# Quads of heads: K and Q loaded in rows of 1,024 and 1,536 bytes, token order restored on chip, bounds in three column groups, and a new order of the work

## The chip, the cores and the metric

The kernel runs on one core of one Trainium2 chip. The metric is device time in microseconds (us). The core has five engines with instruction queues of their own: TensorE (PE in the profile; PEld is its weight load), VectorE (DVE), ScalarE (ACT), GpSimd (POOL) and SyncE (SP). Data comes from device memory (HBM) into the on-chip memory (SBUF, 128 partitions) through 16 DMA engines that are started by DMA instructions in a queue, nearly all of them in SP's. TensorE writes its results to PSUM.

## The reference, cut to what matters

Four batches, eight heads, 768 tokens, head size 64. Keys are grouped in 24 chunks of 32 tokens. For each query and each chunk an upper bound of the score is formed from the chunk's smallest and largest key; the six chunks with the highest bounds (among those that do not lie in the future) are kept, and ordinary causal softmax attention runs over the kept chunks. The result goes through a two-layer block with a hard-swish between the layers.

```python
k_min, k_max = np.min(k_chunks, axis=3), np.max(k_chunks, axis=3)          # chunks of 32 tokens
ub = np.sum(np.maximum(q[:, :, :, None, :] * k_min[:, :, None, :, :], q[:, :, :, None, :] * k_max[:, :, None, :, :]), axis=-1)
top_chunks = np.argsort(np.where(causal, ub, -1e9), axis=-1)[..., -6:]
scores = np.where(sel & (pos[:, None] >= pos[None, :]), scale * np.matmul(q, k.transpose(0, 1, 3, 2)), -1e9)
attn_out = softmax(scores) @ v                                             # (4, 8, 768, 64)
h = x @ w_in                                                               # x: (3072, 512), w_in: (512, 2048)
out = (h * np.clip(h + 3, 0, 6) / 6) @ w_out                               # (3072, 512) float32
```

A query's first six chunks need no choice, so for the first 192 tokens of a head no bounds are computed.

## The kernel before

Everything is written into one list of tokens, `ORDER`, a hand-over from a planner: each token names an operation and its arguments, and the program issues them from left to right. Each engine works off its own tokens strictly in this order; a token that has to wait holds up all later tokens of the same engine. The list is thus five queues in one.

**Pairs and quads.** Heads are processed in pairs i = 0 to 15 (two heads, four pairs per batch). Pairs 0 to 3 (the first batch) take one path, written with capital letters: K and Q arrive in halves (`LK`, `LQ` on SP, `AQ` on ACT's queue, 96 KB each), are turned by TensorE against an identity matrix (`KT`, `QT`), cast (`KB`, `QB`) and reduced to chunk bounds (`MX`, `MN`); `UH`, `UB`, `TH`, `T8`, `SE`, `LH`, `MT` give the selection. Pairs 4 to 15 are taken as quads n = 2 to 7 (four heads, two pairs each), written with small letters, and these are what the change is about:

- `lk.n`, `lq.n` (line 222, SP): load K or Q of four heads into a third of `STAGE`, 768 KB. Head g of the quad goes to partitions 32g to 32g+31; a row of one token (64 floats, 256 bytes) is one piece. Four DMA instructions, one for each head.
- `kd`, `qd` (line 228, DVE): transpose 32x32 blocks in place, in two halves of 128x768. Afterwards a partition holds one of 32 dimensions and the free axis runs over chunk n, half x of the head size and token t.
- `kb`, `qb` (line 303, ACT): cast to bfloat16 into `KBA`, `QBA`, two instructions of 128x768 each. `mx`, `mn` (line 311, DVE): the largest and smallest key of each chunk, two instructions each. `kx` (line 316, DVE): largest minus smallest. `rp` (line 322, ACT): the positive part of Q.
- `ud` (line 333, PE): the bounds, as 64 float32 matmuls on 32x32 tiles: two operands w (positive part, raw Q), two halves x, four column groups `part` of 144 queries, four heads g. The results stand in 128 partitions (4 groups of 32 chunks) by 144 queries. Each matmul shows as two records.
- `us` (339), `tr` (343), `tm` (350, nine instructions per half quad), `se` (353), `tb` (357), all DVE: add the causal bias, transpose, find the eight largest of each list, compare with the sixth, transpose back. `mv` (line 363, POOL): 16 copies per quad gather the mask of each head into one row block `MQ`.
- `SQ` (lines 510 and 514, PE): scores of a quad; line 510 multiplies K by Q, line 514 adds the mask with a matmul whose moving operand is read from `MQ` in runs of eight.
- `ex` (520, ACT) and `af` (527, POOL): exponent and causal cut; `A`, `B` (543, PE) multiply by V, loaded by `LV` or `lv` (SP) and cast by `VC` or `vc` (POOL); `na`, `nb` (560, 563, DVE) normalise into `XB`.

**The block behind it.** A group of 384 tokens is transposed either by TensorE (`X`, line 576) and copied by DVE (`xe`, 580), or by DMA (`xt`, 569); groups 0 to 2 take the first way, groups 3 to 7 the second. `H` (587, PE) is a piece of the first layer, eight matmuls of 384 columns; `hu` (595, ACT) and `gt` (598, DVE) form the hard-swish; `O` (625, PE) is a quarter of a tile of the second layer, four matmuls of 512 columns; `ot` (632, ACT) and `st` (636, SP) bring it out. The weights come in eight loads of 1 MB (`wl`, line 238, SP) into two buffers `WS` in turn and are cast by POOL (`wc`, 242), so `wl.2` waits for `wc.0` and so on.

**Queues around the change.** On SP the tokens from the first quad load on are, before:

```
lk.2 LV.3.0.0 LK.3.1.1 LV.0.0.1 LV.1.0.1 LQ.3.1.0 LV.1.0.0 LQ.3.1.1 LV.2.0.0 LV.2.0.1 LV.0.1.1 wl.0 wl.1 LV.0.1.0 LV.1.1.1 LV.1.1.0 wl.2 lk.3 wl.3 lq.2 LV.3.1.0 LV.3.1.1 LV.2.1.1 LV.2.1.0 wl.4 lq.3 wl.5 wl.6 lv.5 wl.7 lk.4 lq.4 lv.4 st.0.0 lv.7 st.0.1 st.0.2 lv.6 lk.5 lv.8 st.1.0 lq.5
```

On PE the first quad's bounds `ud.2` stand behind all scores and value products of pairs 0 to 3 and all of `H.0`; `ud.3` behind `H.1` but two pieces; `ud.4` behind `A.4`.

Of the kernel before, what the change touches and what calls it, by code (L numbers as in the profile page):

```python
# [15 lines left out]
P = 128  # L16
CH = 32
# [17 lines left out]
PW AQ.2.0.1 LK.0.0.0 PT PI PO LK.0.1.1 AQ.0.0.1 PR Z.y.6 PZ PF PB LK.0.0.1 KT.0.0.b PC AQ.0.0.0 MX.0.0 EG.2 LK.1.0.1  # L35
MN.0.0 EG.0 LK.1.0.0 PA EG.1 QT.0.0.y AQ.1.0.1 EG.3 AQ.1.0.0 LK.0.1.0 AQ.2.0.0 RP.0.0 RN.0.0 KT.1.0.a MN.1.0 MX.1.0
KB.0.0 QB.0.0 QT.1.0.x KT.0.1.y RP.1.0 KB.1.0 RN.1.0 UH.0.0.c UH.1.0.b QB.1.0 MN.0.1 KB.0.1 LQ.0.1.1 UB.1.0 UB.0.0
MX.0.1 LQ.0.1.0 QT.0.1.a RA.0.1 QB.0.1 RP.0.1 TH.1.0.b T8.1.0 TH.0.0.c LQ.3.0.1 T8.0.0 QT.2.0.x RP.2.0 SE.1.0
LQ.3.0.0 QT.3.0.y RP.3.0 LK.3.0.0 RN.2.0 SE.0.0 LK.2.0.1 UH.0.1.a LK.2.0.0 KT.2.0.b RN.3.0 LK.3.0.1 UB.0.1 QB.2.0
MN.2.0 QB.3.0 KT.3.0.c LQ.2.1.0 KB.3.0 LH.1.0.a MX.2.0 MT.1.0 KB.2.0 LQ.2.1.1 QT.2.1.y UH.2.0.a RP.2.1 RA.2.1 QB.2.1  # L40
MX.3.0 LK.3.1.0 LH.0.0.b MN.3.0 TH.0.1.x LQ.1.1.1 MT.0.0 S.0.1.b ex.0.1 UB.2.0 T8.0.1 SE.0.1 S.0.0.a ex.0.0 LK.1.1.0
af.0.0 LQ.1.1.0 QT.1.1.c RN.1.1 QB.1.1 TH.2.0.y RP.1.1 LH.0.1.b LK.1.1.1 KT.1.1.x T8.2.0 SE.2.0 UH.3.0.a LH.2.0.y
MT.0.1 LV.3.0.1 KB.1.1 LV.0.0.0 LK.2.1.1 S.1.1.b UB.3.0 ex.1.1 af.1.1 MT.2.0 MN.1.1 S.0.5.c LK.2.1.0 MX.1.1 KT.2.1.y
MN.2.1 MX.2.1 S.1.0.a TH.3.0.x ex.0.5 ex.1.0 UH.1.1.b T8.3.0 S.2.1.c SE.3.0 UB.1.1 UH.2.1.a UB.2.1 af.0.5 LH.3.0.b
MT.3.0 TH.1.1.x af.0.1 ex.2.1 KB.2.1 af.2.1 T8.1.1 S.2.0.c TH.2.1.y af.1.0 ex.2.0 lk.2 LV.3.0.0 S.0.3.b ex.0.3
S.0.4.c SE.1.1 T8.2.1 SE.2.1 LH.1.1.x MT.1.1 LK.3.1.1 ex.0.4 LV.0.0.1 VC.0.0 KT.3.1.a MN.3.1 A.0.y LV.1.0.1 na.0
# [646 lines left out]
```

## Time and profile before

| what | us |
|---|---|
| time, median of 2 runs (276.49 to 276.76) | 276.62 |
| the profiled execution, its own time | 275.69 |
| its span, first to last instruction | 274.0 |
| PE busy | 261.3 (95%) |
| DVE busy | 184.0 (67%) |
| ACT busy | 181.0 (66%) |
| POOL busy | 102.6 (37%) |
| SP's DMA queue, share of 16 engines | 56.6% |

Busy time is the time that an engine's records cover. The profile's groups give line, engine, operation, tile, shape and count, then busy time, mean nanoseconds of one, and the idle time before the group with what ended it. The chain is followed back from the last instruction to what released it. A stretch (window) gives each engine's busy time in it, the granted clock, the mean busy share of the 16 DMA engines and the GB/s that they moved. The granted TensorE clock is 1.000 all through.

### The profile page before, as it was taken

To read this page: it belongs to the slowest core of one execution; us is meant where nothing else is said; L and a number is where in the kernel's file an instruction comes from. 1 tells how busy PE (TensorE), PEld (TensorE's weight loads), DVE (VectorE), ACT (ScalarE), POOL (GpSimd) and SP (SyncE) were. 2 spreads that over 40 slices of the span, in tenths; PEclk is the share of its full clock that TensorE was granted. 3 is DMA by queue.
4 is the path that set the end of the run, shared out by engine and by line. 5 is a ranking of instruction groups with operands and counts; after the bars stand their busy time and mean duration, and the time that the engine had idled before them with its cause. 6 is when DMAs were issued, how large, how long until landed. Compare 5 with 4: busy or idle time off the path is not lost.

```text
span 274.0 us, 8574 instructions
## 1 busy us (share of the span) xinstructions
PE 261.3 (95%) x3550; PEld 153.7 (56%) x3550; DVE 184.0 (67%) x452; ACT 181.0 (66%) x249; POOL 102.6 (37%) x241
## 2 busy tenths in 40 slices
PE   6998997899999999999999999998999999999994
PEld 3666765565545565664545655464655565555561
DVE  4898998999899779867874788575662423342620
ACT  2798978647499894878578746992887634325610
POOL 7215686325777552532825232421544310000000
PEclk9999999999999999999999999999999999999999
DMA  8999999998996999139900449114212044003002
GB/s 164 205 180 163 335 250 252 219 286 246 261 184 190 160 212 186 36 76 171 231 4 28 107 103 173 40 21 99 79 52 47 2 133 100 0 2 115 38 22 97
DMA packets 91479, 36.08 MB, mean 132 GB/s; under 512 B 84144, under 2 KB 84400, under 8 KB 91440
## 3 DMA queue, kind: packets, MB, share of 16 engines
q1 hardware_dynamic: 89040, 34.94, 56.6%
q10 hardware_dynamic: 2400, 0.59, 1.2%
q8 instruction: 28, 0.46, 0.8%
q14 instruction: 11, 0.09, 0.1%
HBM read 27.26 MB, written 6.29 MB: 122 GB/s over the span
## 4 chain that ended last, share of the span: by engine, by line
PE 76%; DMA 13%; SPq 3%; DVE 3%; POOL 1%; ACT 1%; issue 1%; DVEq 0%
PE PSy L625 15%; PE PSx L625 10%; PE PBa L587 10%; PE PBc L587 9%; PE PBb L587 8%; DMA WS<-in_moe_w_in_dram 4%; DMA STAGE<-in_q_dram 4%; DMA STAGE<-in_k_dram 3%; PE PBa L510 3%; PE PSx L543 2%; PE PSy L543 2%; PE PBc L625 2%; PE PBc L510 2%; PE PBb L510 2%; PE PBb L333 2%; DMA XT<-XB 1%
## 5 line engine op out<-in xcount | busy, mean ns | idle before, releaser
L587 PEld LDWEIGHTS <-WIN 128*128 128x128 bf16 x512 | 48.9, 98 | 37.7 <-issue 4.2
L527 POOL TENSOR_SCALAR_AFFINE_SELECT PT<-PT 128x256 bf16<-128x256 bf16 x78 | 30.2, 409 | 70.2 <-ACT PT L520 69.9
L625 PEld LDWEIGHTS <-GT 128*128 128x128 bf16 x368 | 33.1, 98 | 37.8 <-issue 2.4
L625 PE MATMUL PSy<-WOUT,GT 128*128 128x512 bf16 x192 | 46.8, 380 | 0.0
L363 POOL COPY MQ<-MTM 32x144 bf16<-32x144 bf16 x96 | 29.1, 304 | 31.3 <-DVE MTM L357 27.5
L587 PE MATMUL PBc<-XT,WIN 128*128 128x384 bf16 x184 | 33.7, 326 | 1.4 <-DVE GT L598 1.4
L598 DVE SCALAR_TENSOR_TENSOR GT<-U,PBa 128x768 bf16<-128x768 bf16 x22 | 20.9, 948 | 19.8 <-ACT U L595 19.8
L587 PE MATMUL PBa<-XT,WIN 128*128 128x384 bf16 x176 | 32.4, 326 | 1.3 <-DMA XT<-XB 0.7
L625 PE MATMUL PSx<-WOUT,GT 128*128 128x512 bf16 x128 | 31.8, 380 | 0.0
L598 DVE SCALAR_TENSOR_TENSOR GT<-U,PBc 128x768 bf16<-128x768 bf16 x23 | 21.8, 947 | 10.4 <-ACT U L595 10.3
L520 ACT ACTIVATE PT<-PBb 128x1024 bf16<-128x1024 f32 (+2 forms) x26 | 23.6, 908 | 7.6 <-PE PBb L514 5.3
L587 PE MATMUL PBb<-XT,WIN 128*128 128x384 bf16 x152 | 27.8, 326 | 0.2 <-POOL WIN L242 0.2
L595 ACT ACTIVATE U<-PBc 128x768 bf16<-128x768 f32 x23 | 18.7, 812 | 13.9 <-PE PBc L587 10.2
L598 DVE SCALAR_TENSOR_TENSOR GT<-U,PBb 128x768 bf16<-128x768 bf16 x19 | 18.1, 951 | 13.6 <-ACT U L595 13.6
L595 ACT ACTIVATE U<-PBa 128x768 bf16<-128x768 f32 x22 | 17.9, 812 | 13.5 <-PE PBa L587 13.5
L520 ACT ACTIVATE PT<-PBc 128x1024 bf16<-128x1024 f32 (+2 forms) x26 | 24.2, 930 | 3.5 <-PE PBc L497 1.3
L520 ACT ACTIVATE PT<-PBa 128x1024 bf16<-128x1024 f32 (+2 forms) x26 | 23.9, 921 | 3.8 <-PE PBc L514 2.0
L228 DVE STREAM_TRANSPOSE STAGE<-STAGE 128x768 f32<-128x768 f32 x24 | 22.7, 960 | 1.7 <-DMA STAGE<-in_k_dram 1.3
L595 ACT ACTIVATE U<-PBb 128x768 bf16<-128x768 f32 x19 | 15.4, 812 | 12.1 <-PE PBb L587 12.1
L311 DVE TENSOR_REDUCE KMA<-STAGE 128x24 f32<-128x768 f32 x24 | 22.3, 941 | 0.1
L543 PEld LDWEIGHTS <-PT 128*128 128x128 bf16 x546 | 19.0, 97 | 3.6 <-issue 0.7
L510 PEld LDWEIGHTS <-KBA 32*128 32x128 bf16 x480 | 9.4, 92 | 14.7 <-issue 11.7
(192 smaller groups left out, 460.3 us busy)
## 6 DMA issues: line engine op xcount, KB each, us to landing
out_dram<-OT SPq DMA_DIRECT2D x23, 256.0 KB, 2.5
STAGE<-in_k_dram SPq DMA_DIRECT2D x24, 192.0 KB, 5.0
STAGE<-in_q_dram SPq DMA_DIRECT2D x24, 192.0 KB, 5.5
VS<-in_v_dram SPq DMA_DIRECT2D x12, 384.0 KB, 4.2
WS<-in_moe_w_in_dram SPq DMA_DIRECT2D x4, 1024.0 KB, 7.0
WS<-in_moe_w_out_dram SPq DMA_DIRECT2D x4, 1024.0 KB, 6.7
STAGE<-in_k_dram SPq DMA_DIRECT2D x16, 96.0 KB, 3.2
VS<-in_v_dram SPq DMA_DIRECT2D x16, 96.0 KB, 4.2
```

The lines of the kernel that those rows point to most:

```text
L228: nc.vector.transpose(out=T, in_=T)
L311: nc.vector.tensor_reduce(out=dst, in_=staged("k", n)[:, h], axis=AX.X, op=(A.max, A.min)[w])
L333: nc.tensor.matmul(PSB[(c, cc)[g // 2]][CH * part:CH * (part + 1), g % 2, 0:NQ // 4], lhsT=KM4[n % 2][rows, w, x, :], rhs=R[rows, :, x, 8 ...
L363: nc.gpsimd.tensor_copy(MQ[n % 2][CH * g:CH * (g + 1), w * part:w * (part + 1)], MT4[n % 2][CH * part:CH * (part + 1), w * g:w * (g + 1)])
L510: nc.tensor.matmul(PSB[both[g // 2]][:, g % 2, at:at + w], lhsT=K[rows, x, j * P:(j + 1) * P], rhs=Q[rows, x, q0:q0 + w], start=(x == 0), ...
L520: nc.scalar.activation(pt(i, u)[:, :, 0:n], PSB[slot["S", i, u]][:, :, 0:n], ACT.Exp, scale=float(scale))
L527: nc.gpsimd.affine_select(out=T[:, :, lo:lo + P], in_=T[:, :, lo:lo + P], pattern=[[0, 2], [1, P]], compare_op=A.is_ge, fill=0.0, base=0, ...
L543: nc.tensor.matmul(O[:, e, t, :], lhsT=pt(i, u)[:, e, lo:lo + P], rhs=VB[i % 4][:, j, e, :], start=(j == 0), stop=(j == qb))
L587: nc.tensor.matmul(PSB[c][:, ff, 0:GRP], lhsT=WIN[:, kt, (2 * f + ff) * P:(2 * f + ff + 1) * P], rhs=XT[g % 3][:, kt, :], start=(kt == 0), ...
L595: nc.scalar.activation(slot["R", g, f][:], PSB[slot["H", g, f]][:, :, 0:GRP], ACT.Relu, bias=3.0)
L598: nc.vector.scalar_tensor_tensor(out=GT[g % 2][:, 2 * f:2 * f + 2, :], in0=slot["R", g, f][:], scalar=6.0, in1=PSB[slot["H", g, f]][:, :, ...
L625: nc.tensor.matmul(PSS[c], lhsT=GT[g % 2][:, f, t * P:(t + 1) * P], rhs=WOUT[:, f, :], start=(f == 0), stop=(f == FT - 1))
```

## The change

It is made for quads only, but for three things that touch the pairs of the first batch or the end: the late half of the pairs' bounds is laid out anew, group 2 is transposed by DMA (`xt.2` in place of `X.2.0`, `X.2.1`, `xe.2.0`, `xe.2.1`), and the list `ORDER` is another permutation of the same tokens.

- **Loads.** `RUN` says how many consecutive tokens form one piece: 4 for K (1,024 bytes), 6 for Q (1,536 bytes). A DMA instruction takes, for one u, 32 pieces of each of four heads, and writes all 128 partitions: 6 instructions for K and 4 for Q in place of 4 and 4, with 128 pieces each. Its source runs over heads (4), then pieces (32), then the row; its destination over 128 partitions, then the row.
- **Token order.** After the transposes the free axis runs over u, r (which token of the piece), x and t. `kb`, `qb` read it with r innermost, at a step of 64 floats, and become four instructions of 128x384 each; `mx`, `mn` read runs of eight tokens for each r and become four instructions each.
- **Bounds.** `ud` has three column groups of 192 queries, 48 matmuls; `us`, `tr`, `se`, `tb` run on 96 partitions by 384 in place of 128 by 288; `tm` has twelve instructions per half quad; `mv` is 12 copies of 32x192 per quad and restores token order for Q (reads at a step of 32); line 514's counterpart reads `MQ` in one run.
- **Pairs, late half.** `UH.i.1` is 16 matmuls of 96 columns in four groups in place of 8 of 192, `UB` one add of 128x192 in place of 64x384, `TH` two transposes in place of four.
- **Order.** On SP, from the first quad load on, after:

```
lk.2 LQ.3.1.0 LQ.3.1.1 wl.0 LV.0.0.0 LV.0.0.1 LV.2.0.0 LV.1.0.1 LV.1.0.0 LV.3.0.1 LV.2.0.1 LV.3.0.0 lk.3 LV.0.1.1 LV.1.1.1 LV.0.1.0 wl.1 LV.1.1.0 wl.2 wl.3 LV.3.1.1 LV.2.1.1 LV.2.1.0 lq.2 LV.3.1.0 wl.4 lq.3 wl.5 wl.6 lv.5 wl.7 lq.4 lk.4 lv.4 lk.5 lv.7 st.0.0 st.0.2 lv.6 lq.5
```

On PE, `ud.2`, `ud.3` and `ud.4` stand behind the same work as before, in another sequence.

```diff
+    RUN = {"k": 4, "q": 6}
+    NP3 = NQ // 3
...
+    def slab(m, n):
+        at = (1 + 2 * (n - FIRST_QUAD) + "kq".index(m)) % 3
+        return FLAT[:, 2 * S * at:2 * S * (at + 1)]
+
     def staged(m, n):
-        at = (1 + 2 * (n - FIRST_QUAD) + "kq".index(m)) % 3
-        return STAGE[:, 2 * at:2 * at + 2].rearrange("p h (n x t) -> p h n x t", x=2, t=CH)
+        return slab(m, n).rearrange("p (u r x t) -> p x u r t", r=RUN[m], x=2, t=CH)
...
     def load_rows(m, x):
-        def issue(n, *only):
+        def issue(n):
             b, first = divmod(4 * n, H)
-            dst = staged(m, n).rearrange("p h n x t -> p (h n) (x t)")
-            for g in only or range(4):
-                nc.sync.dma_start(dst[CH * g:CH * (g + 1)], x[b, first + g].rearrange("(n t) d -> t n d", t=CH))
+            r = RUN[m]
+            dst = slab(m, n).rearrange("p (u y) -> p u y", y=r * D)
...
+                src = x[b, first:first + 4].rearrange("g (u t r) d -> u g t (r d)", t=CH, r=r)
+                for u in range(S // (CH * r)):
+                    nc.sync.dma_start(dst[:, u], src[u])
...
     def to_bf16(m, engine):
         def issue(n, h):
...
+                for x in range(2):
+                    copy(dst[:, x, us], staged(m, n)[:, x, us].rearrange("p u r t -> p u t r"))
...
     def chunk_bounds(w):
         def issue(n, h):
-            dst = KM4[n % 2][:, w, :, NCH // 2 * h:NCH // 2 * (h + 1)].rearrange("p x n -> p n x")
-            nc.vector.tensor_reduce(out=dst, in_=staged("k", n)[:, h], axis=AX.X, op=(A.max, A.min)[w])
...
+            for x in range(2):
+                nc.vector.tensor_reduce(out=dst[:, x].rearrange("p (u c) -> p u c", c=c),
+                                        in_=src[:, x, us * h:us * (h + 1)].rearrange("p u r (c t) -> p u c r t", c=c),
+                                        axis=AX.XY, op=op)
...
     def bounds(n, c, cc):
...
-                for part in range(4):
+                for part in range(3):
                     for g in range(4):
                         rows = slice(CH * g, CH * (g + 1))
-                        nc.tensor.matmul(PSB[(c, cc)[g // 2]][CH * part:CH * (part + 1), g % 2, 0:NQ // 4],
-                                         lhsT=KM4[n % 2][rows, w, x, :], rhs=R[rows, :, x, 8 * part:8 * part + 8],
+                        R = raw[rows, x, 6 * part + 6:6 * part + 12] if w else RPA[rows, x, NP3 * part:NP3 * (part + 1)]
+                        nc.tensor.matmul(PSB[(c, cc)[g // 2]][CH * part:CH * (part + 1), g % 2, 0:NP3],
+                                         lhsT=KM4[n % 2][rows, w, x, :], rhs=R,
...
     def top8(n, p):
-        for s in range(9):
-            nc.vector.max(out=T8D[:, 9 * p + s, :], in_=bounds_rows(p)[:, s, :])
+        for s in range(12):
+            nc.vector.max(out=T8D[0:96, 12 * p + s, :], in_=bounds_rows(p)[:, s, :])
...
     def gather_rows(n, g):
-        for part in range(4):
-            w = NQ // 4
-            nc.gpsimd.tensor_copy(MQ[n % 2][CH * g:CH * (g + 1), w * part:w * (part + 1)],
-                                  MT4[n % 2][CH * part:CH * (part + 1), w * g:w * (g + 1)])
+        for part in range(3):
+            lo = NP3 * part
+            src = MT3[(2 * n + g // 2) % 3][CH * part:CH * (part + 1), NP3 * (g % 2):NP3 * (g % 2 + 1)]
+            dst = MQ[n % 2][CH * g:CH * (g + 1), lo:lo + NP3]
+            if RUN["q"] > 1:
+                src, dst = src.rearrange("p (r t) -> p t r", t=CH), dst.rearrange("p (t r) -> p t r", t=CH)
+            nc.gpsimd.tensor_copy(dst, src)
...
     def bounds_half(i, h, c):
-        n = 96 * (h + 1)
         for m, R in enumerate((RP, RN)):
-            for g in range(2):
-                lo = Q0 * h + n * g
+            for g in range(2 * (h + 1)):
+                lo = first_query(h, g) - Q0
...
     def scores_quad(n, u, *both):
-        chosen = MQ[n % 2][:].rearrange("p (r n t) -> p n r t", r=4, t=8)
...
-                                 rhs=chosen[rows, (lo - Q0) // CH:(q0 + w - Q0) // CH], start=False, stop=True,
+                                 rhs=MQ[n % 2][rows, lo - Q0:q0 + w - Q0], start=False, stop=True,
```

More of the change, by code (lines that the diff above doesn't have):

```diff
@@ L108 @@
+O.7.2.2.y O.7.2.3.y ot.7.2 st.7.2 st.7.1 st.7.0
 """.split()
@@ L284, in zero_masks @@
         nc.vector.memset(EM[:], 0.0)
[L285 removed]
+        nc.vector.memset(BIAS3[:], 0.0)
     def spread(g):
@@ L366, in bias_quad @@
     def bias_quad():
-        for g in range(4):
-            T = BIAS4[CH * g:CH * (g + 1)]
-            nc.gpsimd.affine_select(out=T, in_=T, pattern=[[1, NQ // CH], [0, 8]], compare_op=A.is_ge, fill=-1e9,
-                                    base=TOPK, channel_multiplier=-1)
+        for g in range(3):
+            T = BIAS3[CH * g:CH * (g + 1)]
+            nc.gpsimd.affine_select(out=T, in_=T, pattern=[[1, 6], [6, CH]] if RUN["q"] == 6 else [[CH, 6], [1, CH]], compare_op=A.is_ge, fill=-1e9,
+                                    base=Q0 * (g + 1), channel_multiplier=-CH)
```

253 lines of the change are left out of this document (132 added, 121 removed).

## The prediction

> **What bounds the kernel now.** I read the page first (busy time, DMA queues), then stretches of the span, then the chain of waits in the stretch that the change touches.
>
> ```profile
> PE 261.3 (95%) x3550; PEld 153.7 (56%) x3550; DVE 184.0 (67%) x452; ACT 181.0 (66%) x249; POOL 102.6 (37%) x241
> ...
> q1 hardware_dynamic: 89040, 34.94, 56.6%
> q10 hardware_dynamic: 2400, 0.59, 1.2%
> ```
>
> PE is covered for 261.3 of 274.0 us: only 12.7 us can be won by filling it. The stretches show where those are (columns: busy time of PE, PEld, DVE, ACT, POOL with counts, granted clock, DMA share, GB/s):
>
> ```profile
> 0.00:16.80 16.80, 13.17 (x133) 8.57 (x134) 12.03 (x52) 9.54 (x23) 7.14 (x17) 1.00 0.96 182
> 16.80:52.30 35.50, 31.83 (x489) 21.84 (x488) 32.70 (x89) 29.22 (x40) 21.05 (x38) 1.00 1.01 235
> 52.30:69.90 17.60, 17.17 (x272) 10.84 (x269) 16.98 (x40) 11.35 (x17) 8.03 (x13) 1.00 0.96 259
> 69.90:89.20 19.30, 19.30 (x328) 9.99 (x330) 17.32 (x44) 14.84 (x21) 14.53 (x36) 1.00 0.94 217
> 89.20:113.20 24.00, 24.00 (x444) 14.55 (x444) 20.50 (x53) 18.97 (x26) 9.08 (x23) 1.00 0.88 165
> 113.20:274.00 160.80, 155.83 (x1898) 87.86 (x1896) 84.43 (x177) 97.07 (x128) 42.77 (x117) 1.00 0.33 74
> 250.00:260.00 10.00, 10.00 (x62) 5.87 (x60) 5.88 (x7) 6.83 (x9) 0.00 (x0) 1.00 0.28 105
> ```
>
> Up to 52.3 us the DMA engines are taken all the time (0.96, 1.01) and PE is not; from there to 89.2 both are full; after 113 the DMA share is 0.33. So **the first 52 us belong to the DMA queue**, and from then on PE sets the pace. The chain of waits has the hand-over:
>
> ```profile
> 42.00 0.59 SPq L222
> ...
> 44.62 7.67 DMA STAGE<-in_q_dram
> ...
> 52.42 0.98 DVE STAGE L228
> ...
> 54.16 0.97 DVE STAGE L228
> 55.13 0.02 issue
> 55.15 0.53 ACT RPA L322
> 55.68 0.04 issue
> 55.73 0.31 PE PBc L333 x2
> ...
> 57.74 0.46 PE PSx L576 x6
> ```
>
> `lq.2`, the first Q quad, lands at 52.29; two transposes and the positive part later, `ud.2` starts at 55.73. From landing to start: 3.44 us. The other two marks that I need are the starts of `ud.3`, `ud.4` and `ud.5` on PE, and the DVE work from the first transpose of K's third quad to its span (`kd.4.1` to `kx.4`):
>
> ```profile
> 69.92 0.31 PE L333 MATMUL PBb<-RPA,KMA 32*32 32x144 f32 x2
> ...
> 89.16 0.31 PE L333 MATMUL PBb<-RPA,KMA 32*32 32x144 f32 x2
> ```
>
> ```profile
> 114.17 0.31 PE L333 MATMUL PBb<-RPA,KMA 32*32 32x144 f32 x2
> ```
>
> ```profile
> 80.71 0.93 DVE L228 STREAM_TRANSPOSE STAGE<-STAGE 128x768 f32<-128x768 f32 x1
> ...
> 87.98 0.46 DVE L316 TENSOR_TENSOR KMA<-KMA 128x48 f32<-128x48 f32 x1
> ```
>
> **The change part by part. Loads.** A quad load is 786,432 bytes. Up to 16.8 us only 256-byte rows are moved: 182 / 0.96 = 190 GB/s, 11.9 for each of 16 engines. From 250 to 260 us only stores, in 2,048-byte rows: 105 / 0.28 = 375 GB/s, 23.4 for each. So a quad load costs 4.1 us of all engines now, and longer rows on 16 engines would cost 2.1 to 4.1.
>
> But on how many engines does it run? ACT's queue q10 answers that for the transfers of before: it carries six half loads of 384 rows, 2,304 packets, and shows 2,400. The 96 left are 16 for each load, one closing packet per engine; the outermost size of those loads is 128 on both sides. The quad loads of before have 32 outermost on both sides. The new ones have **four heads outermost in the source** and 128 partitions in the destination. If shares are cut along the outermost size, four shares can be made, and a load lies on four engines while twelve stand by. No row shows a load with so small an outermost size, so both ends stay: 16 engines (2.1 to 4.1 us) or four, 196,608 bytes each, 8.4 us at the 23.4 GB/s of 2,048-byte rows, 16.6 at the 11.9 of the short ones. I take four engines and 9.0 us, near the long rows.
>
> The Trainium skill ("DMA: Bandwidth & Descriptors", section "Why a DMA increments its semaphore by 16 and not by 1") says that a DMA is spread over the largest count up to 16 that divides the slowest dimension of both sides, on the lowest-numbered engines. By that rule it is four engines, the same four each time; the 16 closing packets above agree with it for 128, and no run here shows it for four.
>
> *Step A, `ud.2`.* Three quad loads (`lk.2`, `lk.3`, `lq.2`) lie before 52.3 in a queue that is never empty: 3 x (9.0 - 4.1) = 14.7 us on the engines that end last. `LV.3.1.1`, `LV.2.1.1`, `LV.2.1.0` now stand ahead of `lq.2`: 98,304 bytes at 190 GB/s, 0.5 each, 1.6. `lq.2` lands at 52.3 + 16.3 = 68.6, `ud.2` starts at 72.0. The work ahead of `ud.2` on PE is the same set of operations as before and was done at 55.7, so nothing covers the wait: **+16.3**. Weights and V are spread over all engines, so their shares on the four end behind the quad loads too; `H.0` gets its weights later by as much, and no work is left over to fill in.
>
> *Step B, `ud.4`.* After `lq.2` come one V half (0.5), four weight loads (2.8 each at 375 GB/s, 11.2), `lv.5` (2.1) and three quad loads (27.0): `lk.4` lands at 109.4. From 80.71 to 88.44 DVE needed 7.7 us for transposes, reductions and span; with eight half-size reductions some 8.3. `ud.4` can start at 117.7. Pushed by step A alone it would stand at 89.16 + 16.3 = 105.5: **+12.2** more. `ud.3` between them isn't late: `lq.3` lands at 68.6 + 0.5 + 2.8 + 9.0 = 80.9, `ud.3` starts at 69.92 + 16.3 = 86.2. Nor is `ud.5`: `lk.5` and `lq.5` (18.0), three `lv` (6.3) and two stores (1.4) end at 135.1, plus 3.4, against 114.17 + 28.5 = 142.7. Behind it a quad takes over 30 us of PE and 18 of the four engines, and the share was 0.33: hidden.
>
> *What is queued behind the loads.* On SP:
>
> ```profile
> L222 SPq DMA_DIRECT2D STAGE<-in_k_dram x24: 311/520/2432, 15.3 to 126.6; - x24
> ```
>
> ```profile
> 81.27 0.37 SPq L636 DMA_DIRECT2D out_dram<-OT  x1
> ```
>
> Twelve more DMA instructions at 0.31 to 0.52 are 4 to 6 us of SP in the whole run, four of them before `lq.2`: 2.1, behind a queue that isn't empty, so nothing. At the end `st.7.1` now follows `st.7.2`: one issue more behind the last tile, +0.4. On DVE `kd.2.0` now stands ahead of the selection of pairs 1 to 3 and waits for `lk.2` (issued near 17, landed near 27); up to 3 us of DVE and then PE, covered by the wait for `lq.2`, which ends at 72. `kd.5.1` stands ahead of `us.4` and waits for `lk.5` (120.5): 1 to 2 us, covered by pieces of `O`. Without these covers both would add their time.
>
> **The engines' own work.**
>
> ```profile
> L363 POOL COPY MQ<-MTM 32x144 bf16<-32x144 bf16 x96 | 29.1, 304 | 31.3 <-DVE MTM L357 27.5
> ...
> L311 DVE TENSOR_REDUCE KMA<-STAGE 128x24 f32<-128x768 f32 x24 | 22.3, 941 | 0.1
> ...
> L350 DVE MAX8 T8D<-UBT 128x8 f32<-128x32 f32 x108 | 11.0, 176 | 0.3
> ...
> L303 ACT CAST KBA<-STAGE 128x768 bf16<-128x768 f32 x12 | 9.9, 832 | 0.0
> ...
> L343 DVE STREAM_TRANSPOSE UBT<-UBM 128x288 f32<-128x288 f32 x12 | 5.6, 466 | 0.1
> ...
> L288 POOL COPY EM<-XT 32x768 bf16<-32x768 bf16 x4 | 3.3, 818 | 0.2
> ...
> L412 DVE TENSOR_REDUCE KMA<-PSy 128x12 f32<-128x384 f32 x4 | 2.1, 553 | 0.3 <-PE PBc L440 0.3
> ...
> L576 PE MATMUL PSx<-IDENTB,XB 128*128 128x128 bf16 x12 | 1.0, 221 | 0.0
> ...
> L405 ACT CAST KBA<-PSy 128x384 bf16<-128x384 f32 x2 | 1.0, 476 | 0.3 <-DVE KMA L412 0.3
> ```
>
> ```profile
> L510 PE MATMUL PBb<-QBA,KBA 32*128 32x384 bf16 x88 | 10.9, 326 | 0.0
> ...
> L514 PE MATMUL PBb<-MQ,EM 32*128 32x384 bf16 x36 | 5.9, 321 | 0.0
> ```
>
> - DVE: 24 reductions of 941 ns become 48 of about 553: +3.9 us. Four kinds of 12 instructions go from 288 to 384 columns; by the transpose (466 ns at 288, 0.93 us at 768 in the rows above) that is 0.1 each, +4.8. `tm` 108 to 144 at 11.0 / 108: +3.7. About +12 of 184, spread over 200 us, beside matmuls. Of it 1.2 lies before 57 us, under the DMA.
> - ACT: 24 casts of 832 become 48 of 476 to 832 (a step of 64 floats isn't in the trace; contiguous, or twice the price per element): +2.9 to +20 of 181. I take the lower; a cast is not on the way to `ud`.
> - POOL: 72 copies for 96 of 304 ns (29.1 us in all); by the 818 for 768 columns, 343 each, 24.7; at twice that, 49: still half of POOL idle, and 16 us of PE work stand between bounds and mask.
> - PE: the mask reads in one run, but reading runs of eight was no dearer (321 beside 326): 0. The bounds have the same column count, 64 x 144 = 48 x 192, and took 57.7 - 55.7 = 2.0 us: from 3/4 (priced by instruction) to 4/3 (12 tiles in flight in place of 16), -3 to +4 in six quads; I take 0. `X.2` goes: two times six transposes of 0.5, -1.0.
> - The late quads let `gt` and `ot` catch up where DVE was 90% busy: -1.0, an estimate.
>
> **Sum.** 275.69 + 16.3 + 12.2 + 0.4 - 1.0 - 1.0 = 302.6 for the profiled execution; the median stood 0.9 above it: 303.5, **303** as a round number. At 8.4 us a load both steps give 24.9, 300; with step B hidden 289; at 11 us 40.5, 316. Its own range is 289 to 316.
>
> **Rivals.** *All 16 engines, DVE takes over (within 2%).* Three loads of about 2.5 save 4.8 before `lq.2`, V takes 1.6 back; but DVE is busy for 32.70 of 35.5 us there and gets 1.2 more, so 1.6 to 3.2 remain, and 1.0 of `X.2`: about 273. For it: the queue's share of 1.01. Against it: the four heads outermost.
> *All 16 engines, faster by over 2%.* The place is `lq.2` at 52.29; its price at the full 375 GB/s is 3 x 2.0 - 1.6 = 4.4, plus 1.0, 271. It decides only if, beside that, the new order takes over 1 us of DVE work out of the first 52 us: 269.
> *All 16 engines, strided reads at twice the price.* The 16 reductions of the first two quads cost 0.94 like whole ones, +7.5 on a DVE that idles 3.4 us from 16.8 to 69.9: 281.
> *The loads are cut to four engines but land in time*, because PE's work was late anyway: against it stand 55.7 for PE's work and 52.29 for the landing; it is the 289 end.
>
> **How the numbers follow.** Four engines 0.70 (nearly all slower), 16 engines within 2% 0.15, faster 0.10, strided 0.05. 2% is 5.5 us, about what a measurement of this kernel can tell from no change. Slower 0.74, same 0.15, faster 0.11. The range reaches from 271 to 316: it leaves out the faster rival and the upper tail of the first.
>
> **What would show it.** Four engines: landings of K and Q quads near 9 us and more, the DMA share between 20 and 110 us well under 0.9 while DVE and PE wait for `STAGE`, PE idle just before the bounds near 60 to 72 us and again near 110. 16 engines: landings under 5 us and `ud.2` before 55 us. The number of packets tells too: per load 4 or 16 closing ones. I am wrong if the compiler cuts the source otherwise, or if the four engines are faster than 23.4 GB/s.

## The result, and the profile after

The changed kernel takes **324.38 us** (median of 2 runs, 323.69 to 325.08) against 276.62: a ratio of 1.173, 95% interval 1.162 to 1.184. It is slower by 47.8 us, more than the forecast of 303 and its range (to 316). The profiled execution took 325.08 us, its span is 322.6. Left out of the numbers below are three executions, one of the seventh experiment and two of the tenth, that took far longer than the others of the same kernel.

The page of the kernel after, cut to the rows that answer to those of before (busy time; PE's busy tenths, granted clock and DMA share in 40 slices; packets and SP's queue):

```profile
PE 274.8 (85%) x3402; PEld 158.0 (49%) x3402; DVE 190.2 (59%) x510; ACT 198.7 (62%) x273; POOL 108.7 (34%) x218
...
PE   4898849783999578989994799399999999999994
...
PEclk9599959979699999999999599789999999999999
DMA  8948497669424374915227049900251003130112
...
DMA packets 63397, 36.44 MB, mean 113 GB/s; under 512 B 48384, under 2 KB 56320, under 8 KB 63360
...
q1 hardware_dynamic: 60960, 35.33, 44.0%
```

PE's busy time is 13.5 us longer with nearly the same work, and 47.8 us of the span are without PE work where it was 12.7. The granted clock, 1.0 all through before, falls to half in several slices. DMA runs short of work: stretches of after, with the bounds used for before (busy time of PE, PEld, DVE, ACT, POOL with counts, granted clock, DMA share, GB/s):

```profile
16.80:52.30 35.50, 27.87 (x511) 19.89 (x496) 27.31 (x101) 25.59 (x40) 16.77 (x32) 0.89 0.66 198
52.30:69.90 17.60, 14.16 (x189) 9.42 (x192) 12.97 (x24) 10.72 (x15) 6.22 (x8) 0.90 0.60 165
69.90:89.20 19.30, 14.14 (x158) 7.82 (x130) 12.24 (x28) 10.93 (x15) 5.06 (x4) 0.82 0.74 202
```

Before, the DMA share was 1.01, 0.96 and 0.94 there. Now it is 0.60 to 0.74, while DVE and PE wait for the loads. The waits of after (engine, line, what it waited for: us in all, times, longest):

```profile
DVE STAGE L237 <- DMA STAGE<-in_k_dram: 21.3, 4, 8.3
...
DVE STAGE L237 <- DMA STAGE<-in_q_dram: 9.5, 2, 6.1
...
PE PBc L615 <- DVE GT L626: 6.3, 2, 6.1
PE PBa L615 <- DMA XT<-XB: 5.9, 1, 5.9
PE PSy L571 <- DVE XB L591: 5.7, 2, 5.5
...
PE PBc L615 <- DVE UBM L363: 5.2, 1, 5.2
```

Line 237 is `kd` and `qd`, the transposes of the quads: 30.8 us of waiting, where line 228 of before had 1.7. The last four rows are the long waits of PE, in front of line 615 (`H`) or 571 (`A`, `B`); in three of them what PE waits for comes from DVE, which is late. The bounds `ud.2` to `ud.7` start, in the timeline of PE, at

```profile
69.58 0.35 PE L357 MATMUL PBb<-RPA,KMA 32*32 32x192 f32 x2
...
91.08 0.35 PE L357 MATMUL PBb<-RPA,KMA 32*32 32x192 f32 x2
...
114.65 0.35 PE L357 MATMUL PBa<-RPA,KMA 32*32 32x192 f32 x2
...
145.63 0.35 PE L357 MATMUL PBa<-RPA,KMA 32*32 32x192 f32 x2
...
195.77 0.35 PE L357 MATMUL PBb<-RPA,KMA 32*32 32x192 f32 x2
...
231.24 0.35 PE L357 MATMUL PBb<-RPA,KMA 32*32 32x192 f32 x2
```

and those of `ud.6` and `ud.7` of before at

```profile
155.76 0.31 PE L333 MATMUL PBc<-RPA,KMA 32*32 32x144 f32 x2
...
185.53 0.31 PE L333 MATMUL PBc<-RPA,KMA 32*32 32x144 f32 x2
```

With the starts that the prediction quotes, the lag is 13.9 us at `ud.2`, 21.2 at `ud.3`, 25.5 at `ud.4`, 31.5 at `ud.5`, 40.0 at `ud.6`, 45.7 at `ud.7` and 48.6 at the end. About half of it comes after `ud.4`, where the prediction let it stop. How one such wait is made, in the chain of waits of after (start, length, what):

```profile
64.43 14.19 DMA STAGE<-in_q_dram
78.62 0.02 issue
78.65 0.98 DVE STAGE L237
79.62 0.46 DVE UBM L370
80.08 0.45 DVE UBM L363
80.53 0.04 issue
80.58 2.72 PE PBc L615 x8
...
88.12 1.30 PE PBc L615 x8
```

`lq.3` lands at 78.62. `ud.3`, for which it was loaded, starts only at 91.08; but `qd.3.1` stands in DVE's queue ahead of `us.2.1` (line 363), which frees the bank that `H.1.6` needs. So PE waits, though the bounds of quad 3 are 12 us off. And when it starts again, eight matmuls that last 1.30 us elsewhere take 2.72.

The groups of after that changed (line, engine, operation, tiles, shape, count, busy us, mean ns of one):

```profile
L394 POOL COPY MQ<-MTM 32x192 bf16<-32x192 bf16 x72 | 36.0, 500 | 39.8 <-DVE MTM L384 37.0
L333 DVE TENSOR_REDUCE KMA<-STAGE 128x12 f32<-128x384 f32 x48 | 23.4, 541 | 0.1
...
L320 ACT CAST KBA<-STAGE 128x384 bf16<-128x384 f32 x24 | 19.7, 890 | 0.0
L320 ACT CAST QBA<-STAGE 128x384 bf16<-128x384 f32 x24 | 19.5, 873 | 0.0
```

The casts take 39.2 us where they took 19.8.

### The profile page after: what moved, and what is told of

Its sections match the earlier page's. It is cut to its first block, busy times and chain, and to the rows that moved or that the text cites. A ratio compares the mean times of both kernels' runs of the same rounds, so it can differ in the third digit from the quotient of the medians.

```text
span 322.6 us, 8358 instructions
## 1 busy us (share of the span) xinstructions
PE 274.8 (85%) x3402; PEld 158.0 (49%) x3402; DVE 190.2 (59%) x510; ACT 198.7 (62%) x273; POOL 108.7 (34%) x218
## 2 busy tenths in 40 slices
DMA packets 63397, 36.44 MB, mean 113 GB/s; under 512 B 48384, under 2 KB 56320, under 8 KB 63360
## 4 chain that ended last, share of the span: by engine, by line
PE 54%; DMA 17%; DVE 9%; ACT 8%; SPq 6%; POOL 3%; issue 2%; ACTq 0%; DVEq 0%; POOLq 0%
PE PSy L653 9%; PE PBc L615 9%; DMA STAGE<-in_q_dram 6%; PE PBa L615 6%; PE PSx L653 6%; PE PBb L615 5%; DMA VS<-in_v_dram 4%; ACT PT L548 3%; DVE GT L626 3%; DMA STAGE<-in_k_dram 3%; SPq L231 2%; DMA WS<-in_moe_w_in_dram 2%; PE PBa L653 2%; DMA XT<-XB 2%; ACT U L623 2%
## 5 line engine op out<-in xcount | busy, mean ns | idle before, releaser
L615 PEld LDWEIGHTS <-WIN 128*128 128x128 bf16 x512 | 51.4, 102 | 59.7 <-issue 23.1
L615 PE MATMUL PBc<-XT,WIN 128*128 128x384 bf16 x200 | 40.4, 349 | 11.5 <-DVE GT L626 6.3
L394 POOL COPY MQ<-MTM 32x192 bf16<-32x192 bf16 x72 | 36.0, 500 | 39.8 <-DVE MTM L384 37.0
L615 PE MATMUL PBa<-XT,WIN 128*128 128x384 bf16 x184 | 37.2, 350 | 7.2 <-DMA XT<-XB 5.9
L237 DVE STREAM_TRANSPOSE STAGE<-STAGE 128x768 f32<-128x768 f32 x24 | 23.1, 967 | 30.8 <-DMA STAGE<-in_k_dram 21.3
L548 ACT ACTIVATE PT<-PBa 128x1024 bf16<-128x1024 f32 (+2 forms) x28 | 26.8, 959 | 8.7 <-POOL WIN L251 7.6
L626 DVE SCALAR_TENSOR_TENSOR GT<-U,PBc 128x768 bf16<-128x768 bf16 x25 | 23.6, 946 | 10.9 <-ACT U L623 10.9
L626 DVE SCALAR_TENSOR_TENSOR GT<-U,PBb 128x768 bf16<-128x768 bf16 x16 | 15.2, 950 | 19.0 <-ACT U L623 19.0
L615 PE MATMUL PBb<-XT,WIN 128*128 128x384 bf16 x128 | 23.6, 327 | 0.2 <-DVE GT L626 0.2
L333 DVE TENSOR_REDUCE KMA<-STAGE 128x12 f32<-128x384 f32 x48 | 23.4, 541 | 0.1
L320 ACT CAST KBA<-STAGE 128x384 bf16<-128x384 f32 x24 | 19.7, 890 | 0.0
```

Source lines behind the costliest of these rows:

```text
L237: nc.vector.transpose(out=T, in_=T)
L320: copy(dst[:, x, us], staged(m, n)[:, x, us].rearrange("p u r t -> p u t r"))
L333: nc.vector.tensor_reduce(out=dst[:, x].rearrange("p (u c) -> p u c", c=c), in_=src[:, x, us * h:us * (h + 1)].rearrange("p u r (c t) -> p ...
L394: nc.gpsimd.tensor_copy(dst, src)
L548: nc.scalar.activation(pt(i, u)[:, :, 0:n], PSB[slot["S", i, u]][:, :, 0:n], ACT.Exp, scale=float(scale))
L615: nc.tensor.matmul(PSB[c][:, ff, 0:GRP], lhsT=WIN[:, kt, (2 * f + ff) * P:(2 * f + ff + 1) * P], rhs=XT[g % 3][:, kt, :], start=(kt == 0), ...
```

## The experiments

Each time is a median; the ratio is to the kernel before on the same chip, with its 95% interval. Differences between experiments are taken from the ratios, times 276.6.

**1. The same loads, cut by heads.** The row lengths stay, the outermost size becomes 32 on both sides.

```diff
-                src = x[b, first:first + 4].rearrange("g (u t r) d -> u g t (r d)", t=CH, r=r)
-                for u in range(S // (CH * r)):
-                    nc.sync.dma_start(dst[:, u], src[u])
+                for g in range(4):
+                    nc.sync.dma_start(dst[CH * g:CH * (g + 1)],
+                                      x[b, first + g].rearrange("(u t r) d -> t u (r d)", t=CH, r=r))
```

> The changed kernel with one edit: a quad load is four DMA instructions, one for each head, onto 32 partitions, with 32 pieces outermost in the source, still 1,024- and 1,536-byte rows; all else stays, the strided reads, the three column groups and the new order too. Theory F (the loads lie on four of 16 engines and that is nearly the whole loss): 276 to 286 us, quad landings under 5 us, 18 us of dearer casts on ACT mostly hidden, 16 closing packets for each load. Rival O (the new order, or the dearer engine work, is the loss): above 305 us. Rival S (strided reads): 295 to 310 us.

Measured: 287.73 us, ratio 1.039 (1.033 to 1.046): 36.9 us of the 47.8 are gone, though it stays 1.7 us above the span that theory F gave. Packets and the stretches of this kernel:

```profile
DMA packets 63925, 36.44 MB, mean 128 GB/s; under 512 B 48912, under 2 KB 56848, under 8 KB 63888
```

```profile
52.30:69.90 17.60, 15.56 (x233) 10.37 (x233) 15.18 (x35) 13.86 (x19) 7.31 (x6) 1.00 1.01 296
69.90:89.20 19.30, 18.50 (x255) 9.36 (x257) 18.41 (x61) 15.83 (x23) 12.22 (x23) 1.00 0.86 180
```

The DMA share is back at 1.01 and the clock at 1.00. The packets give the number of engines: 48 load instructions with 16 closing packets each leave 63,925 - 768 = 63,157 for all else, and 63,397 - 63,157 = 240 is four for each of the 60 instructions of the changed kernel. In the packet records the 512 packets of a Q quad follow each other within 8.6 to 11.2 us in the changed kernel and within 4.0 to 5.7 us here; one packet lasts 65 ns there (median), 110 here. Four engines are faster each and far slower together.

**2. Short rows.** Rows of 256 bytes, contiguous reads; the three column groups and the new order stay.

```diff
-    RUN = {"k": 4, "q": 6}
+    RUN = {"k": 1, "q": 1}
```

> The changed kernel with rows of one token again (256 bytes, one instruction per head, 32 tokens outermost), so that no read is strided; three column groups and the new order stay. F: 276 to 284 us, within 5 us of the run with long rows by head: the row length is worth little once 16 engines carry it. S: at least 8 us below that run, since 18 us of ACT and 11 us of POOL go. O: above 300 us.

Measured: 281.21 us, ratio 1.017 (1.012 to 1.022), 6.2 us less than the first experiment, between what the two theories gave. Long rows on 16 engines are no gain but a loss; the sixth and eleventh experiments find where.

**3. The first experiment in the order of before.** Only the list `ORDER` is exchanged.

> As the run with long rows by head, but with the order list of before (group 2 transposed on TensorE again). F: 274 to 286 us, within 5 us of the new order. O: at least 10 us below the new order.

Measured: 286.41 us, ratio 1.035 (1.029 to 1.041): not told apart from the first experiment. The new order neither causes nor heals the loss there.

**4. The new order alone**, in the kernel before (the list `ORDER` is exchanged, and the late half of the pairs gets a second buffer, which that order needs):

```diff
-    T8D = const.tile([P, 2 * HQ // CH, 8], FP32, name="T8D")
-    T8H = [[T8D[0:96, 4 * n:4 * n + 4] for n in range(2)], [T8D[0:96, 8:16]] * 2]
+    T8D = const.tile([P, 24, 8], FP32, name="T8D")
+    T8H = [[T8D[0:96, 4 * n:4 * n + 4] for n in range(2)], [T8D[0:96, 8 * n + 8:8 * n + 16] for n in range(2)]]
```

> The kernel before with the new order list alone (and a buffer of its own for the second late half of the eight largest). F: 272 to 282 us: the order by itself is worth nothing measurable either way. O: above 290 us.

Measured: 282.42 us, ratio 1.021 (1.015 to 1.026), just above the expected span. With the kernel's old layout the new order costs 5.7 us. In the profiled execution, whose span is 7.6 us longer, `ud.2` starts at 61.4 in place of 55.7: 5.7 of the 7.6 lie ahead of the first bounds.

**5. Fillers in the waits.** 300 small matmuls on constants ahead of the pieces that wait at 75, 173 and 201 us, to tell whether the half clock has a price.

```diff
+    def filler(c, n):
+        for _ in range(n):
+            nc.tensor.matmul(PSB[c][:, 0, 384:512], lhsT=IDENTB[:], rhs=WIN[:, 0, 0:P], start=True, stop=True)
...
-gt.1.1 qd.3.0 H.1.6.c
+gt.1.1 qd.3.0 ZF.a.90 H.1.6.c
...
-H.3.3.a lk.6 H.3.6.c
+H.3.3.a lk.6 ZF.b.105 H.3.6.c
...
-xt.4 H.4.4.a
+xt.4 ZF.a.105 H.4.4.a
```

> The changed kernel with 300 small matmuls more (128 columns of constants into banks that the next group overwrites), put on TensorE ahead of the groups that wait for late loads at 75, 173 and 201 us, so that it isn't idle in those waits; nothing else is changed. Theory C: after each of these waits the granted clock stays at 0.5 for 6.8 us, which costs 3.4 us each, 10 in all; with TensorE kept busy the clock stays at 1.0 there and the time falls by 5 to 10 us, to 314 to 319. Rival N (the half clock lies beside work that binds anyway, or the fillers delay as much as they save): 322 to 328.

Measured: 327.5 us, ratio 1.186 (1.180 to 1.192), as rival N had it; but for another reason. The first 90 could not run in their wait (their bank was still held by `H.1.3`, behind the same DVE queue) and came after it: `ud.3` is 5.7 us later than in the changed kernel. From `ud.5` to `ud.6` and from `ud.6` to `ud.7`, where the fillers did run in the waits, the kernel is 1.8 and 2.1 us shorter. The tenth puts the first group right.

**6. and 11. Contiguous casts and mask copies.** The first experiment with casts that write in staged order (both), and with mask copies that do too (the sixth only). The casts still read runs of 32 floats, no longer single floats at a step of 64. Token order is not restored.

```diff
-            dst = (KB4 if m == "k" else QB4)[n % 2].rearrange("p x (u t r) -> p x u t r", t=CH, r=RUN[m])
+            dst = (KB4 if m == "k" else QB4)[n % 2].rearrange("p x (u r t) -> p x u r t", t=CH, r=RUN[m])
...
-                    copy(dst[:, x, us], staged(m, n)[:, x, us].rearrange("p u r t -> p u t r"))
+                    copy(dst[:, x, us], staged(m, n)[:, x, us])
...
-            if RUN["q"] > 1:
-                src, dst = src.rearrange("p (r t) -> p t r", t=CH), dst.rearrange("p (t r) -> p t r", t=CH)
```

> The per-head loads of the first experiment (16 engines, rows of 1,024 and 1,536 bytes), but the casts read and write in the order in which the staged rows lie, and the mask copies on GpSimd too; the token order is not restored, so the output is not the reference's. Theory S (the 6.5 us between long rows and 256-byte rows are the price of the strided reads): the casts and copies last as with 256-byte rows (850 and 340 ns), and the time falls from 287.7 to 280 to 283. Rival L (the price is that of the long rows themselves, in their landings): 286 to 289.

> The sixth experiment with the mask copies on GpSimd strided again (500 ns): only ScalarE's casts read and write in the staged order; the token order is not restored there, so the output is not the reference's. Theory A (the 7.0 us of the strided reads are ScalarE's 48 longer casts, 17 us of work): 280 to 283. Rival G (they are GpSimd's 72 longer copies, 11.5 us of work): 286 to 289.

Measured: 280.68 us, ratio 1.015 (1.013 to 1.017), for the sixth; 281.28 us, ratio 1.016 (1.011 to 1.021), for the eleventh. The groups of the eleventh:

```profile
L394 POOL COPY MQ<-MTM 32x192 bf16<-32x192 bf16 x72 | 36.4, 505 | 29.9 <-DVE MTM L384 27.0
L320 ACT CAST KBA<-STAGE 128x384 bf16<-128x384 f32 x24 | 11.1, 532 | 0.0
L320 ACT CAST QBA<-STAGE 128x384 bf16<-128x384 f32 x24 | 11.1, 522 | 0.0
```

So the casts alone are worth (1.0393 - 1.0161) x 276.6 = 6.4 us, and the mask copies, 11.9 us shorter in the sixth (340 ns for 505), 0.4 us, which is not told from nothing. Theory A holds.

**7. The three column groups without the new order**: the second experiment in the order of before. The new layout of the pairs' late half stays in it too, so it isn't the column groups alone.

> The changed kernel with rows of 256 bytes loaded head by head, contiguous reads, three column groups, and the order of the kernel before: the three column groups alone. Theory O (the 1.7 per cent of the same kernel in the new order come from the order): 274 to 279. Rival G (the three column groups cost it): 280 to 284.

Measured: 279.47 us (middle of 278.79 to 280.45), ratio 1.011 (1.008 to 1.014). That is 3 us above the kernel before, within the 2% that tell no change, and at the boundary of the two theories. There is no profile of one of these three executions, so where the 3 us lie stays open.

**8. Two heads a load.** The suspected cost doubled.

```diff
-                src = x[b, first:first + 4].rearrange("g (u t r) d -> u g t (r d)", t=CH, r=r)
-                for u in range(S // (CH * r)):
-                    nc.sync.dma_start(dst[:, u], src[u])
+                for a in range(2):
+                    src = x[b, first + 2 * a:first + 2 * a + 2].rearrange("g (u t r) d -> u g t (r d)", t=CH, r=r)
+                    for u in range(S // (CH * r)):
+                        nc.sync.dma_start(dst[2 * CH * a:2 * CH * (a + 1), u], src[u])
```

> The changed kernel with every quad load cut in two by heads: twice as many DMAs, each with two heads as its outermost dimension, 64 partitions and the same rows. Theory F (the outermost dimension sets how many of the 16 DMA engines carry a DMA): two engines, landings of about 18 us in the place of 9, two closing packets for each DMA, and 370 to 430 us. Rival Q (a price of the queue or of the rows, not of the engines): 320 to 330.

Measured: 409.72 us, in one execution. The 512 packets of a Q quad take 15.9 to 18.5 us; the count of packets and the wait of the transposes are

```profile
DMA packets 63398, 36.45 MB, mean 89 GB/s; under 512 B 48384, under 2 KB 56320, under 8 KB 63360
```

```profile
DVE STAGE L238 <- DMA STAGE<-in_k_dram: 62.3, 4, 22.6
```

Twice as many instructions and, but for one of 63,398, the same number of packets: two closing packets each (120 x 2 = 60 x 4). Halving the outermost size halves the engines and doubles the landing. Theory F holds.

**9. The late quads by heads.** Quads 5 to 7 load as in the first experiment, quads 2 to 4 as in the changed kernel.

```diff
-            if r == 1:
+            if n > 4:
                 for g in range(4):
-                    nc.sync.dma_start(dst[CH * g:CH * (g + 1)], x[b, first + g].rearrange("(u t) d -> t u d", t=CH))
+                    nc.sync.dma_start(dst[CH * g:CH * (g + 1)], x[b, first + g].rearrange("(u t r) d -> t u (r d)", t=CH, r=r))
```

> The changed kernel with the loads of quads 5, 6 and 7 cut by heads (16 engines, as in the first experiment), and those of quads 2, 3 and 4 as in the changed kernel (four engines). Theory L (the late landings cost time in every stage, the three last quads' too): from the bounds of quad 4 to the end the changed kernel takes 322.6 - 145.6 = 177.0 us and the first experiment 284.1 - 122.5 = 161.6, so the time falls by about 15, to 307 to 311. Rival H (the prediction: behind the bounds of quad 4 the late loads are hidden): 322 to 326.

(The 145.6 and 122.5 us named there are the starts of the bounds of quad 5, not of quad 4; from those of quad 4 on the difference of the two kernels is 16.4.) Measured: 308.15 us, ratio 1.116 (1.107 to 1.125): (1.1727 - 1.1158) x 276.6 = 15.7 us less than the changed kernel. The intervals of the two ratios make that some 4 us uncertain either way; in the profiled executions the stretch from the bounds of quad 4 to the end is 16.8 us shorter (191.2 for 208.0), and the bounds of quads 2 to 4 start within 0.9 us of those of the changed kernel. Theory L holds; the late loads of the last three quads are not hidden.

**10. and 12. Fillers, the first group in a free bank.** `ZF.y.90` in place of `ZF.a.90`; the twelfth is the same kernel again, for its trace.

> The kernel with 300 small matmuls again, but the first 90 write another bank (the one of the fifth experiment was still held when the wait began, so that they ran behind the wait). Theory C (the half clock behind each wait has a price of its own): the two groups of matmuls that ran inside their waits saved 1.8 and 2.1 us in the fifth experiment, so three save about 6, and the time falls from 324.4 to 316 to 320. Rival N: 323 to 327.

> The kernel of the tenth experiment once more, for its trace stage by stage. Theory C: with the first 90 matmuls inside their wait too, the granted clock is 1.0 behind the three waits, and the stretches from the bounds of quad 3 to those of quad 4, from those of quad 5 to those of quad 6 and from those of quad 6 to those of quad 7 are each about 2 us shorter than in the changed kernel (31.0 between quads 4 and 5 the same): 319 to 322 in all. Rival N: the stretches as long as in the changed kernel, 323 to 326.

(The first stretch named in the second text runs from the bounds of quad 2 to those of quad 3, where these fillers stand.) Measured: 319.66 and 322.43 us in the tenth; 320.27 us (319.91 to 321.24), ratio 1.158 (1.151 to 1.166), in the twelfth, 4.0 us less than the changed kernel. The intervals of these two ratios overlap, so the size of the gain rests on the stretches more than on the times. Stretches from each wait to the next bounds, of the changed kernel:

```profile
75.00:91.10 16.10, 10.94 (x51) 5.22 (x49) 11.86 (x37) 7.73 (x11) 6.78 (x8) 0.79 0.58 162
172.50:195.80 23.30, 17.20 (x217) 8.93 (x215) 16.35 (x33) 13.02 (x18) 8.22 (x19) 0.85 0.33 88
201.00:231.20 30.20, 23.77 (x234) 12.68 (x232) 14.77 (x33) 18.98 (x26) 9.02 (x19) 0.89 0.30 51
```

and of the twelfth:

```profile
75.00:90.30 15.30, 13.88 (x144) 9.55 (x144) 11.36 (x36) 7.78 (x11) 6.19 (x7) 1.00 0.66 180
171.00:193.30 22.30, 21.66 (x301) 11.71 (x299) 17.30 (x34) 18.07 (x25) 8.28 (x19) 1.00 0.37 101
200.00:226.70 26.70, 25.77 (x317) 16.42 (x316) 13.19 (x21) 18.13 (x24) 9.04 (x19) 1.00 0.32 53
```

The clock is 1.00 in all three where it was 0.79, 0.85 and 0.89. Between the bounds the twelfth is 1.0 us shorter from quad 2 to 3 (20.5 for 21.5), 1.4 from 5 to 6 and 2.1 from 6 to 7; the waits themselves remain. Theory C holds, at 1 to 2 us for each wait rather than the 3.4 that 6.8 us at half clock would cost if all of them lay behind the wait and beside work that sets the end.

## Why the prediction was right and wrong

The ratios lay the 47.8 us out: 15.7 from the four engines in quads 5 to 7 (changed kernel less ninth), 21.2 from the four engines in quads 2 to 4 (ninth less first), 6.4 from the casts (first less eleventh), 0.4 from the mask copies (eleventh less sixth), and 4.1 for the sixth against before. These are differences taken in one sequence; another sequence could share them out otherwise. The clock's 4.0 lie within the first two.

- **"Four heads outermost in the source ... a load lies on four engines": right.** Four closing packets for each instruction, two with two heads, and 36.9 us less with 32 outermost. The rule of the Trainium skill ("DMA: Bandwidth & Descriptors", section "Why a DMA increments its semaphore by 16 and not by 1"), the largest count up to 16 that divides the slowest size of both sides, agrees with all three: 4, 2 and 16.
- **"I take four engines and 9.0 us": right.** 8.6 to 11.2 us for a Q quad, 9.3 and 10.1 for the first two K quads.
- **Step A, +16.3 at `ud.2`: near in size, but not by the wait that it named.** Measured 13.9, of which 10.9 are the engines (69.6 less the first experiment's 58.7) and 3.0 are there with 16 engines too. `lq.2` is late, in DVE's hands at 64.7 (forecast 68.6), but `ud.2` does not wait for it: the positive part of Q is ready at 66.55, and PE comes to `ud.2` at 69.58, straight from other work. From the timelines of GpSimd, PE and ScalarE:

```profile
64.86 0.51 POOL L422 CAST VB<-VS 128x384 bf16<-128x384 f32 x1 [7.88 <-DMA VS<-in_v_dram]
...
65.42 1.64 PE L571 MATMUL PBb<-VB,PT 128*128 128x65 bf16 x27 [2.67 <-POOL VB L422]
...
65.71 0.84 ACT L346 ACTIVATE RPA<-STAGE 128x768 f32<-128x768 f32 x1 [2.25 <-DVE STAGE L237]
...
66.87 2.45 PE L615 MATMUL PBa<-XT,WIN 128*128 128x384 bf16 x8
```

  What failed is "The work ahead of `ud.2` on PE is the same set of operations as before and was done at 55.7". That work is held up by the late loads itself: `B.3.0` waits 2.7 us for the V half `LV.3.1.0`, which stands behind `lq.2` on SP, and `H.0.7` behind it takes 2.45 us at half clock. Earlier `kd.3.1` waits 5.5 us on DVE for `lk.3`, with `na.2` behind it, and PE stands still from 39.2 to 44.8 us. How much each of these adds to the 13.9 was not tried.
- **Step B, `ud.4` at +28.5 in all: measured 25.5, by another way.** "`ud.3` between them isn't late" failed. The landing of `lq.3` (78.6; the forecast said 80.9) was held against the start of `ud.3`, and was in time for that. But the first to wait is `qd.3` on DVE, 12 us earlier, with `us.2.1` and then PE's `H.1.6` behind it. Of the 11.6 us that come on top of step A, 7.3 stand before `ud.3`, where the prediction had none. Only the other 4.3 lie where it put them: `kd.4.1` waits for `lk.4` until 107.4, and `ud.4` follows 7.2 us later.
- **"Behind it ... hidden" failed, and is the larger part of the miss: 15.7 us.** A DMA share of 0.33 was read as room. It is a mean; the loads come in pairs, and what waits for them is a queue. `lk.7` reaches DVE late:

```profile
167.06 8.37 DMA STAGE<-in_k_dram
175.45 0.99 DVE STAGE L237
...
178.36 0.85 DVE GT L626
179.25 2.72 PE PBc L615 x8
...
200.62 6.44 DMA XT<-XB
207.19 2.72 PE PBa L615 x8
```

  `kd.7.1` holds `gt` (line 626) behind it, and `gt` the bank that PE needs next; and `xt.4`, a transfer that reads nothing of the quad, is issued behind `lq.7`, whose packets run from 193.7 to 203.1 us, and comes at 207. That it lies behind them on the four engines is argued from these times; that these waits go when quads 5 to 7 lie on 16 engines is shown by the ninth experiment, where PE's longest wait behind the bounds of quad 4 is 1.4 us.
- **ACT, "I take the lower; a cast is not on the way to `ud`": failed, 6.4 us.** The 48 casts cost +19.4 us, the upper of the two ends. Nor does it take `ud` for a cast to count: it keeps ScalarE from `ex` and `hu`. DVE waits 50.7 us for `hu` in the first experiment and 44.6 in the eleventh, and PE 1.8 us for `ex` at line 538 in the first and not at all in the eleventh; which of these waits make up the 6.4 us was not followed. The rival "strided reads at twice the price" had the right mechanism on the wrong engine: the reductions, read in runs of eight floats, cost 541 ns, below the 553 that the prediction took.
- **POOL, at most 49 us and no price: right.** 36.0 us, worth 0.4.
- **The clock was missing**: 4.0 us for the three waits that were filled.
- **The order.** The 1.6 us of V ahead of `lq.2` were the only price put on it. In the sixth experiment, with 16 engines and casts that take nearly as long in all as before (22.3 us for 19.8), `ud.2` starts at 60.9 against 55.7, and 5.1 of the 5.4 us by which its span is longer lie ahead of that. The order alone costs 5.7 us (fourth), the three column groups with the pairs' new late half 3 us (seventh), both together 4.6 (second), and under long rows the order is worth nothing (third). These don't add up, and what of the last 4 us belongs to which stays open. The smaller terms (`X.2`, the late quads, the last store) were not tried by themselves, and none of the versions tried beats the kernel before.

The two terms that the forecast set at nothing, 15.7 and 6.4, make up about the 21 us by which it fell short; its smaller misses (steps A and B too high, the clock and the order too low) nearly cancel. Of the marks that it named, the landings, the DMA share well under 0.9 during the waits and the four closing packets came out. PE is idle near 63 and near 110 us as well, but not just before the bounds: near 63 for the cast of a late V half, near 110 for `ex`. So steps A and B and the late quads went wrong at the same point: each late load was held against the operation that uses its data, and not against the first instruction in a queue that waits for it.

## What to carry to other kernels

Read a DMA's outermost size on both sides before its row length: here longer rows with four heads outermost took 8 to 11 us a load in place of 4 to 6, and the same rows cut by heads would have saved 37 of the 48 us. A late load is to be held against the first instruction in an in-order queue that waits for it, and then against everything that stands behind that one, not against the operation that uses the data; and a mean DMA share of 0.33 is no sign of room for loads that come in pairs on a quarter of the engines. A strided read that repairs an order belongs on the engine that has room: here it cost nothing that could be measured on GpSimd and 6 us on ScalarE.

## What the runs showed of the hardware that was not expected

- **Half clock after a wait.** After PE waits of 5.16, 6.09 and 5.92 us the granted clock is 0.5 for 6.8 us each in the clock records, the first 1.2 to 1.8 us of it still inside the wait, and eight matmuls take 2.72 us in place of 1.30. A wait of 5.55 us that ends at 44.8 has 6.8 us at 0.5 too, 3.2 of them inside it; one wait of 2.7 us was followed by 3.4 us at 0.5, and one of 3.2 us by none. The Trainium skill ("TensorE: Matmul & The Clock Gate", section "Part 1: The HAM clock gate (the "warmup" mystery)") says that PE falls to half rate after an idle window of about 3.4 us and returns after a busy one; the 3.4 and 6.8 us here are one and two such windows. The wait of 2.7 us is shorter than a window, so a wholly idle one is not what it took here. The clock is also 0.50 from 7.4 to 17.7 us in the changed kernel and from 7.7 to 18.0 in the fourth experiment. That the new order causes this stretch isn't shown: the profiled executions of the first and the sixth experiment have the same order and no such stretch, and one execution of the kernel before has a mean clock of 0.982.
- **Filling a wait with useless matmuls pays** 1 to 2 us for each wait of 5 to 6 us, provided that they have a bank that isn't held by the wait itself; where they hadn't, `ud.3` came 5.7 us later.
- **Strided reads.** ScalarE's cast of 128x384 float32 takes 873 to 890 ns when it reads single floats at a step of 64, and 522 to 532 in runs of 32; VectorE's reduction of 128x384 in runs of eight takes 541 ns, no more than one of contiguous rows out of PSUM (546 to 553), though two take 141 ns more than one contiguous reduction of 128x768 (941), and whether that is the second instruction or the runs was not tried; GpSimd's copy of 32x192 bfloat16 at a step of 32 takes 500 ns against 340.
